# First four heads' k as fp32 over SyncE's queue, and lambda times alpha1 spread as one row

## The chip, the cores and the metric

The kernel runs on one core of a Trainium2 chip. The metric is the device time of one execution in microseconds (us). The engines of a core run side by side, each with its own list of instructions in a fixed order: PE (TensorE, matrix products), DVE (VectorE), ACT (ScalarE), POOL (GpSimd) and SP (SyncE, which here only issues transfers). An engine that waits holds up all that stands behind it in its own list. Transfers between main memory and the core's memory are issued by SP, ACT or POOL.

## The reference, cut to what matters

Eight batches, eight heads, 576 positions, head width 64. Each k and v is averaged over groups of 8 positions, so that every query sees 72 keys. The output of the attention goes through an affine MLP block with the token mixing matrix w_tok.

```
k_p = k.reshape(B, H, Sp, pool, D).mean(axis=3)
v_p = v.reshape(B, H, Sp, pool, D).mean(axis=3)
scores = scale * np.matmul(q, k_p.transpose(0, 1, 3, 2))
attn = softmax(scores)
x = np.matmul(attn, v_p)            # to [batch, position, 512]
a1 = alpha1 * x + beta1
tok = np.einsum('ts,bsd->btd', w_tok, a1)
u = x + lam * tok
a2 = alpha2 * u + beta2
ch = np.maximum(a2 @ w_ch1, 0.0) @ w_ch2
out = u + lam * ch
```

alpha1, beta1, alpha2, beta2 and lam are rows of 512 numbers. The kernel scales x by lam times alpha1 before the token mixing, so it needs that product on all 128 partitions.

## The kernel before, in words

The order of all work is written out by hand: what stands first in the program stands first in each engine's list. Three parts follow one another. A start-up loads the first batch and builds constants; the statements after the definitions (lines 806 to 889) do the attention of batch 0, the token mixing of its chunks and the first MLP pieces; then a loop over nine blocks of four chunks (lines 943 to 1019) does the MLP of one block beside the attention of the next batch. In that loop each step has a due time, and the steps are issued in order of due times.

The positions of a head are split in 512 "main" ones, four per partition, and 64 at the end ("rem"), two per partition. Heads are loaded in two groups of four, called u = 0 and u = 1.

For batch 0 the start works like this:
- `load_vector` (line 209) loads lam and beta1 into rows of a tile `vecs`; alpha1 goes into a third row (line 218). `load_rem` (141) loads the end positions of q and k in four transfers, two on SP's queue and two on ACT's. `load_q_bf` (74) and `load_k16` (82) load q and k of four heads on POOL's queue, which turns fp32 into bf16 on the way. `load_v16` (96) does the same for v. `load_k` (88), used for later batches, loads k as fp32, by default on SP's queue.
- `keep_warm` (601) runs matmuls on zeros whose result nobody reads.
- `att_F` (388) transposes q on PE and copies it out on ACT; `att_Frem` (416) does it for the end positions, after `cast_rem` (164) has cast them.
- `att_K` (437) pools k by matmuls with the tile `pool_main`. The output must stand twice, once on each half of the partitions. For batch 0 four matmuls per head do that, each with two neighbouring position columns of k as weights; `double_k` (431) first copies column 0 behind column 3 so that the last pair exists, and makes the same copy for the end positions (`cast_rem_k`, 176). For later batches `sum_k` (181) adds the four positions of a partition in two operations, written twice, and one matmul per head is enough. The result goes into the tile kpT, one half by ACT and one by DVE.
- `spread_lam` (301) puts lam on all partitions: a matmul of a row of ones with the row lam, copied by ACT into `lam_bc`. `spread_al1` (307) does it for alpha1, 256 columns at a time, and DVE multiplies it with lam_bc into `lamal_bc`. `att_X` and `rest_X` (574, 567) multiply the attention's output by lamal_bc.
- `att_S` (486) makes the scores and their exponentials, `first_V` (464) the pooled v, `att_AV` (546) the product of both.
- `more_constants` (291) sets constants with four memsets on DVE. `bias_row` (282) makes lam times beta1.

lam_bc itself is read again only in `scale_w2` (711) and, for the first block, in `mlp_B` (674).

The tiles k16 and k_raw share two buffers, so that a load of batch 1's k waits for the readers of the tile before it in its buffer.

Of the kernel before, what the change touches and what calls it, by code (L numbers as in the profile page):

```python
# [11 lines left out]
ALU = mybir.AluOpType  # L12
AX = mybir.AxisListType

P = 128
SPG = 72
DM = 512
# [6 lines left out]
def kernel(  # L24
# [18 lines left out]
    nc = tc.nc  # L43
# [8 lines left out]
    def gp(name):  # L52
        return psA.tile([P, 512], FP, tag="gp", name=name)
# [11 lines left out]
    st1 = {}  # L65
# [16 lines left out]
    def load_k16(b, u):  # L82

        t = work.tile([P, 4, 5, D], BF, tag="k_raw", bufs=2, name="k16")
        nc.gpsimd.dma_start(out=t[:, :, 0:4].rearrange("p h c d -> p h (c d)"), in_=rows(k, b, u))
        st1[b]["k"][u] = t
# [54 lines left out]
    def load_rem(b, queue=nc.sync, behind=None):  # L141

        raw = work.tile([P, 2, 2, 2, D], FP, tag="rem_raw", bufs=2, name="rem_raw")
        if behind is not None:
            behind.memset(raw[:, :, :, 0, 0:1], 0.0)
        for i, src in enumerate((q, k)):
            for h in range(2):
                (nc.scalar if h and not b else queue).dma_start(
                    out=raw[:, i, h].rearrange("p c d -> p (c d)"),
                    in_=src[b, h::2, 512:576, :].rearrange("a (i c) d -> i a (c d)", c=2))  # L150
        st1[b]["rem_raw"] = raw
# [12 lines left out]
    def cast_rem(b, eng, copy=None, behind=None):  # L164
        raw = st1[b]["rem_raw"]
        rq = work.tile([P, 2, 2, D], BF, tag="rem_q", bufs=2, name="rem_q")
        if behind is not None:
            behind.memset(rq[:, 0, 0, 0:1], 0.0)
        rk = work.tile([P, 2, 2 if b else 3, D], BF, tag="rem_k", bufs=2, name="rem_k")
        (copy or eng.tensor_copy)(out=rq.rearrange("p c h d -> p h c d"), in_=raw[:, 0])  # L170
        twice = [raw[:, 1, :, c].unsqueeze(2).to_broadcast((P, 2, 2, D)) for c in range(2)]
        if b:
            eng.tensor_tensor(out=rk, in0=twice[0], in1=twice[1], op=ALU.add)
        st1[b]["rem"] = rq, rk

    def cast_rem_k(eng):
        raw, rk = st1[0]["rem_raw"], st1[0]["rem"][1]
        eng.tensor_copy(out=rk[:, :, 0:2], in_=raw[:, 1])
        eng.tensor_copy(out=rk[:, :, 2], in_=raw[:, 1, :, 0])
# [20 lines left out]
    lam_bc = const.tile([P, DM], FP, tag="lam_bc", name="lam_bc")  # L200
    lamal_bc = const.tile([P, DM], FP, tag="lamal_bc", name="lamal_bc")
# [3 lines left out]
    vecs = const.tile([65, 3, DM], FP, tag="vecs", name="vecs")  # L205
# [3 lines left out]
    def load_vector(i, src, queue=nc.scalar):  # L209
        queue.dma_start(out=vecs[0:65:64, i], in_=src.unsqueeze(0).to_broadcast((2, DM)))  # L210

    new_batch(0)
    load_vector(0, moe_lam)
    load_rem(0)
    load_q_bf(0, 0)
    load_k16(0, 0)
    load_vector(1, moe_beta1, nc.sync)
    nc.scalar.dma_start(out=vecs[0:1, 2], in_=moe_alpha1.unsqueeze(0))
    start = const.tile([1, 2], FP, tag="start", name="start")
    nc.vector.memset(start, 0.0)  # L220
    nc.scalar.activation(out=start[:, 1:2], in_=start[:, 0:1], func=AF.Exp, bias=0.0, scale=1.0)
# [45 lines left out]
    for i in range(2):  # L267
# [5 lines left out]
    nc.vector.memset(pool_v[:, 64:], 0.0)  # L273
    nc.vector.memset(pool_vr, 0.0)
    nc.vector.memset(vr16, 0.0)
    nc.vector.tensor_scalar(out=pool_v[:, 0:64], in0=pool_main, scalar1=8.0, scalar2=None,
                            op0=ALU.mult)
    nc.vector.tensor_tensor(out=pool_vr[0:32, 64:72], in0=pool_v[0:32, 0:16:2],
# [12 lines left out]
    def more_constants():  # L291
        nc.vector.memset(ones_bf, 1.0)
        nc.vector.memset(ones_lo[0:64], 1.0)
        nc.vector.memset(ones_lo[64:128], 0.0)
        nc.vector.memset(wtT[:, :, S:640], 0.0)
# [2 lines left out]
        behind.memset(al2_bc[:, 0:1], 0.0)  # L298
        nc.sync.dma_start(out=al2_bc, in_=moe_alpha2.unsqueeze(0).to_broadcast((P, DM)))

    def spread_lam():

        ps = gp("ps_bc")
        nc.tensor.matmul(out=ps, lhsT=ones_row, rhs=vecs[0:1, 0])
        nc.scalar.copy(out=lam_bc, in_=ps)

    def spread_al1(half):

        ps = gp("ps_bc")[:, 0:256]
        cols = slice(256 * half, 256 * half + 256)  # L310
        nc.tensor.matmul(out=ps, lhsT=ones_row, rhs=vecs[0:1, 2, cols])
        nc.vector.tensor_tensor(out=lamal_bc[:, cols], in0=lam_bc[:, cols], in1=ps, op=ALU.mult)

    def setup_vectors():
        ps = gp("ps_vec")
# [72 lines left out]
    def att_F(b, hp, copy=nc.scalar.copy):  # L388


        st = st1[b]
        u, r = hp // 2, hp % 2
        if r == 0:
            st["qT"][u] = work.tile([P, 8, P], BF, tag="qT", bufs=4, name="qT")
        if b > 1:
            if r == 0:
                nc.sync.dma_start_transpose(out=st["qT"][u],
                                            in_=st["q"][u].rearrange("p h c d -> p (h c d)"))
            return
        ps_q = gp("ps_q").bitcast(BF)  # L400
        for c in range(4):
            nc.tensor.transpose(  # L402
                out=ps_q[:, 128 * c:128 * c + 128],
                in_=st["q"][u][:, 2 * r + c // 2, 2 * (c % 2):2 * (c % 2) + 2].rearrange(
                    "p c d -> p (c d)"),
                identity=identity_bf)

        def finish(copy):
            copy(out=st["qT"][u][:, 4 * r:4 * r + 4, :],
                 in_=ps_q[:, 0:512].rearrange("p (c t) -> p c t", c=4))  # L410

        if copy is None:
            return finish
        finish(copy)

    def att_Frem(b, copy=None):

        st = st1[b]
        st["rem_qT"] = work.tile([P, 2, P], BF, tag="rem_qT", bufs=2, name="rem_qT")
        if copy is None:  # L420
            nc.sync.dma_start_transpose(out=st["rem_qT"],
                                        in_=st["rem"][0].rearrange("p c h d -> p (c h d)"))
            return
        ps_q = gp("ps_qr").bitcast(BF)
        for c in range(2):
            nc.tensor.transpose(out=ps_q[:, 128 * c:128 * c + 128],
                                in_=st["rem"][0][:, c].rearrange("p h d -> p (h d)"),
                                identity=identity_bf)
        copy(out=st["rem_qT"], in_=ps_q[:, 0:256].rearrange("p (c t) -> p c t", c=2))

    def double_k(u):

        nc.vector.tensor_copy(out=st1[0]["k"][u][:, :, 4], in_=st1[0]["k"][u][:, :, 0])
        if u == 0:
            cast_rem_k(nc.vector)

    def att_K(b, u, copy):

        st = st1[b]
        ps_kp = gp("ps_kp")  # L440
        kp = ps_kp[:, 0:4 * SPG].rearrange("p (h g) -> p h g", g=SPG)
        n, nr = (1, 1) if b else (4, 2)
        for h in range(4):
            for c in range(n):
                nc.tensor.matmul(  # L445
                    out=kp[:, h, 0:64],
                    lhsT=st["k"][u][:, h, c:c + 2].rearrange("p a d -> p (a d)"),
                    rhs=pool_main, start=(c == 0), stop=(c == n - 1))
        for hh in range(2):
            for c in range(nr):  # L450
                nc.tensor.matmul(
                    out=kp[:, hh:4:2, 64:72],
                    lhsT=st["rem"][1][:, hh, c:c + 2].rearrange("p a d -> p (a d)"),
                    rhs=pool_rem.rearrange("p (g u r) -> p u r g", r=2, u=2)[:, u],
                    start=(c == 0), stop=(c == nr - 1))
        if b:
            copy(out=kp_pool[u], in_=kp)
            return
        for a in range(2):
            rows = slice(64 * a, 64 * a + 64)  # L460
            (copy or (nc.scalar.copy, nc.vector.tensor_copy)[a])(
                out=kpT_pool[u][rows, a], in_=kp[rows])
# [138 lines left out]
    def keep_warm(count):  # L601

        ps = psB.tile([P, DM], FP, tag="ch", bufs=2, name="ps_warm")
        for _ in range(count):
            nc.tensor.matmul(out=ps, lhsT=warm[:, 0:P], rhs=warm)
# [204 lines left out]
    for u in range(2):  # L810
        load_k(1, u, queue=nc.gpsimd)
    keep_warm(13)
    att_F(0, 0)
    att_F(0, 1)
    cast_rem(0, nc.vector)
    more_constants()
    keep_warm(1)
    att_Frem(0, nc.scalar.copy)
    keep_warm(1)
    spread_lam()  # L820
    double_k(0)
    att_K(0, 0, None)
    spread_al1(0)
    bias_row(0)
    att_S(0, 0)
    att_S(0, 1)
# [18 lines left out]
    att_S(0, 5)  # L845
    att_AV(0, 4)
    att_S(0, 6)
    spread_al1(1)
    att_AV(0, 5)
    att_X(0, 4, 6, nc.gpsimd, False)  # L850
    att_S(0, 7)
# [91 lines left out]
    for n in range(NBLK):  # L943
# [27 lines left out]
        if n >= FIRST:  # L971
# [22 lines left out]
            else:  # L994
                for m in range(4):
                    todo.append((27.2 if m < 2 else 29.2, lambda m=m: store(n, m)))
        if n == 0:
            todo.append((6.2, lambda: setup_rowsum(4)))
            todo.append((8.3, setup_wtok_odd))
            for g in range(2, 4):  # L1000
                todo.append((4 * g - 0.8, lambda g=g: setup_bias(range(4 * g, 4 * g + 4))))
# [48 lines left out]
```

## Time and profile before

| what | value |
|---|---|
| median of 3 runs | 333.14 us (332.15 to 333.55) |
| profiled execution, its own time | 333.62 us |
| span of that execution, first to last instruction | 331.9 us |
| PE busy | 323.7 us (98%) |
| DVE busy | 233.6 us (70%) |
| ACT busy | 175.7 us (53%) |
| POOL busy | 95.2 us (29%) |
| mean granted clock of PE | 0.995 |

The page also gives the span in 40 slices of 8.3 us. The digits are tenths of busy time; PEclk is the clock that PE was granted, in tenths of full speed.

```profile
PE   7999999999999999999999999999999999999995
DVE  6674289989679969676967796877788783263263
PEclk9799999999999999999999999999999999999999
```

In rows of the timeline the numbers are the start and the length of a group in us, then the engine, the line, the operation, the tile written and the tile read, the shape and the count; in brackets stands the idle time of the engine before it and what ended it. In the chain of waits every piece is start, length and work. A row of a transfer queue gives packets, MB and the share of the 16 transfer engines' time.

### The profile page before, as it was taken

The numbers are of one execution on the slowest core, as the hardware profiler recorded it, in microseconds if no ns is written. First come the engines' busy times: TensorE is split into PE (matmuls) and PEld (weight loads), VectorE is DVE, ScalarE is ACT, GpSimd is POOL, SyncE is SP. The second block draws the span as 40 slices with busy tenths as digits, with TensorE's granted clock in tenths as the row PEclk, the third lists the DMA queues.
The fourth block names the chain that finished last, engine by engine and source line by source line (L and its number), as shares of the span: only waits on it lengthen the run. The fifth ranks groups of instructions, "written<-read, shape, count | busy, mean of one in ns | idle before, by whom it ended". The sixth has DMA issues, their size and how long they took to land.

```text
span 331.9 us, 6477 instructions
## 1 busy us (share of the span) xinstructions
PE 323.7 (98%) x2500; PEld 209.6 (63%) x2531; DVE 233.6 (70%) x485; ACT 175.7 (53%) x322; POOL 95.2 (29%) x110
## 2 busy tenths in 40 slices
PE   7999999999999999999999999999999999999995
PEld 3667864455544576656775677558755866586584
DVE  6674289989679969676967796877788783263263
ACT  3584989448422861388128812682268225703710
POOL 8669828401247011800280027102510200000000
PEclk9799999999999999999999999999999999999999
DMA  8999999966895992499449943996340044004003
GB/s 117 191 217 270 270 209 245 206 148 101 152 243 99 219 181 81 80 232 173 147 109 209 173 136 73 209 187 176 65 136 2 0 65 143 2 0 127 1 32 97
DMA packets 66472, 45.81 MB, mean 138 GB/s; under 512 B 34397, under 2 KB 57061, under 8 KB 66442
## 3 DMA queue, kind: packets, MB, share of 16 engines
q1 hardware_dynamic: 52092, 32.67, 43.3%
q0 software_dynamic: 13824, 12.40, 22.9%
q8 instruction: 20, 0.33, 0.4%
q10 hardware_dynamic: 526, 0.34, 0.4%
q14 instruction: 10, 0.08, 0.1%
HBM read 38.30 MB, written 9.44 MB: 144 GB/s over the span
## 4 chain that ended last, share of the span: by engine, by line
PE 94%; DMA 2%; DVE 1%; issue 1%; POOL 1%; ACT 0%; POOLq 0%
PE ps_h L662 38%; PE ps_w L785 26%; PE ps_tok L614 11%; PE ps_ch L682 8%; PE ps_av L556 3%; PE ps_s L513 2%; DMA k<-in_k_dram 2%; PE ps_kp L445 1%; PE ps_sc L493 1%; PE ps_r L520 1%; PE ps_av L560 1%; PE ps_v L472 0%; PE ps_w L329 0%; PE ps_q L402 0%; DVE u_sb L618 0%
## 5 line engine op out<-in xcount | busy, mean ns | idle before, releaser
L662 PE MATMUL ps_h<-u_fm,w 128*128 128x512 bf16 (+2 forms) x588 | 132.6, 368 | 1.3 <-DVE bias_cols L665 0.2
L669 ACT ACTIVATE H<-ps_h,bias_cols 128x512 bf16<-128x512 f32 x144 | 98.2, 688 | 56.5 <-PE ps_h L662 55.5
L662 PEld LDWEIGHTS <-w 128*128 128x128 bf16 x608 | 65.6, 114 | 49.9 <-issue 2.2
L785 PEld LDWEIGHTS <-H 128*128 128x128 bf16 x560 | 53.5, 98 | 10.8 <-DVE u_sb L803 1.2
L622 ACT CAST u_bf<-u_sb 128x512 bf16<-128x512 f32 x32 | 19.8, 618 | 69.9 <-issue 39.9
L785 PE MATMUL ps_w<-w_l,H 128*128 128x256 bf16 x448 | 53.6, 272 | 0.0
L803 DVE TENSOR_TENSOR u_sb<-u_sb,ps_w 128x512 f32<-128x512 f32 x54 | 36.3, 683 | 17.1 <-PE ps_w L785 17.1
L578 POOL TENSOR_TENSOR xs<-x_tm,lamal_bc 128x512 bf16<-128x512 f32 x12 | 15.9, 1328 | 108.7 <-DVE x_tm L564 108.5
L614 PE MATMUL ps_tok<-xs,wtT 128*128 128x512 bf16 (+3 forms) x194 | 44.6, 380 | 0.4
L618 DVE TENSOR_TENSOR u_sb<-x_tm,ps_tok 128x512 f32<-128x512 f32 (+1 forms) x40 | 27.4, 684 | 9.9 <-PE ps_tok L614 9.8
L564 DVE TENSOR_TENSOR x_tm<-ps_av,rec 128x320 f32<-128x320 f32 x64 | 31.5, 492 | 2.6
L542 ACT ACTIVATE ET<-ps_s 72x512 f16<-72x512 f32 x56 | 32.3, 592 | 0.0
L614 PEld LDWEIGHTS <-wtT 128*128 128x128 bf16 (+3 forms) x200 | 17.4, 100 | 16.0 <-issue 1.1
L562 DVE RECIPROCAL rec<-ps_av 128x5 f32<-128x5 f32 x64 | 12.2, 190 | 16.9 <-PE ps_av L560 16.7
L483 DVE TENSOR_TENSOR v_u<-v_u 72x1024 f32<-72x1024 f32 (+1 forms) x24 | 22.7, 948 | 0.2
L785 PE MATMUL ps_w<-w_t,h_s 128*128 128x256 bf16 x168 | 22.6, 272 | 0.0
L682 PEld LDWEIGHTS <-H 128*128 128x128 bf16 x128 | 11.9, 98 | 13.7 <-issue 0.4
L754 DVE TENSOR_TENSOR H<-H,H 128x1024 bf16<-128x1024 bf16 x14 | 9.7, 690 | 14.3 <-ACT H L669 14.2
L185 POOL TENSOR_TENSOR k_raw<-k_raw 128x512 f32<-128x512 f32 x14 | 18.8, 1341 | 0.9 <-PE ps_ch L682 0.7
L785 PEld LDWEIGHTS <-h_s 128*128 128x128 bf16 x168 | 16.4, 98 | 4.1
L187 POOL TENSOR_TENSOR k_bf<-k_raw 128x512 bf16<-128x512 f32 x14 | 18.5, 1319 | 1.1
L754 DVE TENSOR_TENSOR h_s<-H 128x1024 bf16<-128x1024 bf16 x21 | 14.4, 686 | 6.0 <-ACT H L669 5.8
(148 smaller groups left out, 367.6 us busy)
## 6 DMA issues: line engine op xcount, KB each, us to landing
out_dram<-u_sb SPq DMA_DIRECT2D x29, 256.0 KB
k_raw<-in_k_dram SPq DMA_DIRECT2D x12, 512.0 KB
v_u<-in_v_dram SPq DMA_DIRECT2D x12, 512.0 KB
q_bf<-in_q_dram POOLq DMA_DIRECT2D x16, 256.0 KB, 7.3
w<-in_moe_w_ch_dram POOLq DMA_DIRECT2D x6, 512.0 KB, 12.5
out_dram<-u_sb SPq DMA_DIRECT2D x11, 128.0 KB
w<-in_moe_w_ch_dram POOLq DMA_DIRECT2D x1, 1024.0 KB, 15.0
k_raw<-in_k_dram POOLq DMA_DIRECT2D x2, 512.0 KB, 16.8
```

Source lines behind the costliest of these rows:

```text
L483: nc.vector.tensor_tensor(out=out, in0=t[:, :, 0:width], in1=t[:, :, width:2 * width], op=ALU.add)
L542: nc.scalar.activation(out=o, in_=i, func=AF.Exp, bias=0.0, scale=0.125)
L564: nc.vector.tensor_tensor(out=x[:, 1 - odd:6 - odd, dd:dd + D], in0=av[:, :, 0:64], in1=rec.unsqueeze(2).to_broadcast((P, 5, D)), op=ALU.mult)
L614: nc.tensor.matmul(out=ps_tok[p0:p1], lhsT=wtT[0:kk, at, P * c:P * c + p1 - p0], rhs=xs_pool[i][0:kk, sc, :], start=(sc == 0), stop=(sc == 4))
L618: nc.vector.tensor_tensor(out=s["u"][p0:p1, :], in0=x[p0:p1, 1 + c if c < 4 else 5 - 5 * i, :], in1=ps_tok[p0:p1, 0:DM], op=ALU.add)
L622: nc.scalar.copy(out=s["u_bf"], in_=s["u"])
L662: nc.tensor.matmul(out=ps_h[:, t0:t1 + one], lhsT=w1_of(cc, j), rhs=rhs, start=(cc == 0), stop=(cc == 3))
L669: nc.scalar.activation(out=H4[n, j // 4][:, j % 4, :], in_=ps_h, func=AF.Relu, bias=bias_cols[:, j:j + 1], scale=1.0)
L682: nc.tensor.matmul(out=ps, lhsT=H_of(n, j)[:, 128 * m:128 * m + 128], rhs=(w2l if n else w2)[j // 4][:, j % 4, :], start=(j == 0), stop=(j ...
L754: nc.vector.tensor_tensor(out=o, in0=a, in1=b, op=op)
L785: nc.tensor.matmul(out=ps, lhsT=stat(j), rhs=moving(j), stop=(j == 7), start=(first and (pp == 0 or alone) and j == 0), skip_group_check=True)
L803: nc.vector.tensor_tensor(out=o, in0=o, in1=banks[key, "both"], op=ALU.add)
```

## The change

The loads of batch 0's first group change: k comes as fp32 on SP's queue, as SP's first transfer, and alpha1 is loaded before ACT's two rem transfers. DVE adds k's four positions (`sum_k`), so that `att_K` needs one matmul per head for this group; the second group stays as it was. The product lam times alpha1 is made by DVE on one row, spread by one matmul of 512 columns, and copied by ACT into lamal_bc. lam_bc is no longer filled from PE: a transfer on SP's queue writes it during the first block. more_constants moves behind att_K, one of the warm matmuls goes, and `spread_lamal` stands before `att_Frem`.

```diff
     load_vector(0, moe_lam)
+    nc.scalar.dma_start(out=vecs[0:1, 2], in_=moe_alpha1.unsqueeze(0))
+    load_k(0, 0)
     load_rem(0)
     load_q_bf(0, 0)
-    load_k16(0, 0)
     load_vector(1, moe_beta1, nc.sync)
-    nc.scalar.dma_start(out=vecs[0:1, 2], in_=moe_alpha1.unsqueeze(0))
...
     nc.vector.memset(vr16, 0.0)
+    nc.vector.tensor_tensor(out=vecs[0:1, 2], in0=vecs[0:1, 2], in1=vecs[0:1, 0], op=ALU.mult)
...
-    def spread_lam():
+    def spread_lamal():
         ps = gp("ps_bc")
-        nc.tensor.matmul(out=ps, lhsT=ones_row, rhs=vecs[0:1, 0])
-        nc.scalar.copy(out=lam_bc, in_=ps)
-
-    def spread_al1(half):
-        ps = gp("ps_bc")[:, 0:256]
-        cols = slice(256 * half, 256 * half + 256)
-        nc.tensor.matmul(out=ps, lhsT=ones_row, rhs=vecs[0:1, 2, cols])
-        nc.vector.tensor_tensor(out=lamal_bc[:, cols], in0=lam_bc[:, cols], in1=ps, op=ALU.mult)
+        nc.tensor.matmul(out=ps, lhsT=ones_row, rhs=vecs[0:1, 2])
+        nc.scalar.copy(out=lamal_bc, in_=ps)
+
+    def load_lam(behind):
+        behind.memset(lam_bc[:, 0:1], 0.0)
+        nc.sync.dma_start(out=lam_bc, in_=moe_lam.unsqueeze(0).to_broadcast((P, DM)))
...
     def double_k(u):
-        nc.vector.tensor_copy(out=st1[0]["k"][u][:, :, 4], in_=st1[0]["k"][u][:, :, 0])
         if u == 0:
             cast_rem_k(nc.vector)
+        else:
+            nc.vector.tensor_copy(out=st1[0]["k"][u][:, :, 4], in_=st1[0]["k"][u][:, :, 0])
...
-        n, nr = (1, 1) if b else (4, 2)
+        n, nr = 1 if b or u == 0 else 4, 1 if b else 2
...
     keep_warm(13)
+    sum_k(0, 0, nc.vector)
     att_F(0, 0)
     att_F(0, 1)
     cast_rem(0, nc.vector)
+    double_k(0)
+    keep_warm(1)
+    spread_lamal()
+    att_Frem(0, nc.scalar.copy)
+    att_K(0, 0, None)
     more_constants()
-    keep_warm(1)
-    att_Frem(0, nc.scalar.copy)
-    keep_warm(1)
-    spread_lam()
-    double_k(0)
-    att_K(0, 0, None)
-    spread_al1(0)
     bias_row(0)
...
     att_S(0, 6)
-    spread_al1(1)
     att_AV(0, 5)
...
         if n == 0:
+            todo.append((1.5, lambda: load_lam(nc.vector)))
```

## The prediction

> **What bounds the kernel now.** I read the page's chain of waits by engine and line first, then the same chain in order of time for the first 60 us, then the timeline and the table by stretches around the edit.
>
> ```profile
> PE 94%; DMA 2%; DVE 1%; issue 1%; POOL 1%; ACT 0%; POOLq 0%
> ```
>
> ```profile
> 2.25 6.64 DMA k<-in_k_dram
> 8.93 0.81 PE ps_kp L445 x16
> 9.87 0.40 ACT kpT L461
> 10.29 0.47 DVE kpT L461
> 10.81 0.33 PE ps_sc L493
> ...
> 18.50 0.62 PE ps_bc L311 x2
> 19.12 0.23 PE ps_av L556 x4
> ```
>
> The chain is TensorE for 94% of the span; the one long piece that is not is the load of the first four heads' k, issued at 2.25 and landed at 8.89. From 10.81 on TensorE hands on to itself almost without a break. So a microsecond won before that point, or a matmul taken out behind it, reaches the end. The second spread of alpha1 (L311) is such a matmul: 0.62 us of the chain.
>
> ```profile
> 6.60 0.62 PE L402 MATMUL ps_q<-identity_bf,q_bf 128*128 128x128 bf16 x8 [0.90 <-DMA q_bf<-in_q_dram]
> 7.06 0.38 PE L605 MATMUL ps_warm<-early 128*128 128x512 f16 x1
> 7.70 1.12 PE L304 MATMUL ps_bc<-vecs,ones_row 1*128 1x512 f32 x2
> 8.00 0.39 ACT L429 COPY rem_qT<-ps_qr 128x256 bf16<-128x256 bf16 x1
> 8.85 0.59 ACT L305 COPY lam_bc<-ps_bc 128x512 f32<-128x512 f32 x1 [0.47 <-PE ps_bc L304]
> 9.05 0.29 DVE L178 CAST rem_k<-rem_raw 128x256 bf16<-128x256 f32 x1
> ```
>
> Before k lands, everything else is already done: q is transposed by 7.06, lambda is spread and copied by 9.44. These steps have slack only because k is late.
>
> ```profile
> 11.00:12.00 1.00, 1.00 (x8) 0.88 (x7) 0.89 (x2) 0.86 (x4) 1.00 (x2) 0.50 1.44 187
> 14.00:14.50 0.50, 0.50 (x8) 0.44 (x7) 0.33 (x2) 0.39 (x2) 0.00 (x0) 0.63 1.16 221
> ```
>
> In this table of stretches the third column from the right is the granted clock. It is 0.50 from about 10.95 to 14.37 and full elsewhere after the start: the first scores run at half speed.
>
> **The change, part by part.** Against the profiled run: 333.62 us, of which the span is 331.9 and 1.72 lies around it; it is 0.48 above the median of 333.14.
>
> *When k and q land.* k leaves POOL's queue and becomes SP's first transfer. SP's first transfer now (rem_raw, issued 0.81) moves its first packets at 2.5, so k's 512 packets start there. How fast? In 121 to 126.5 us two such loads (1,024 packets) took 122.5 to 126.2 alone: 277 a microsecond, 1.85 us for one. Beside POOL's queue the hardware queues now get 178 a microsecond (below: 99 and 79), which makes 2.9 us. The last packet is at 4.35 to 5.4. q_bf's 512th packet passes at about 5.55 and it lands at 6.5, a lag of 1.0; so k lands at 5.3 to 6.4, and I take 6.1, nearer the shared rate.
>
> ```profile
> q0 software_dynamic: 257, 0.13, 104.5%
> ...
> q0 software_dynamic: 199, 0.10, 70.7%
> q1 hardware_dynamic: 99, 0.05, 33.6%
> q10 hardware_dynamic: 79, 0.04, 13.2%
> ```
>
> These are the packets of the queues in 3.75 to 4.75 (first line: POOL's queue nearly alone) and in 4.75 to 5.75 (beside SP's and ACT's): POOL's q transfer falls from 257 to 199. With k beside it from 3.75 to 5.1 it loses some 60 packets, 0.25 us: the transposes start at 6.85 instead of 6.60. Bounds: no delay, or k's whole 1.85 us ahead of it, 8.45.
>
> The Trainium skill ("DMA: Bandwidth & Descriptors", section "Issuing engines are not separate DMA queues") says that transfers from SP, ACT and POOL all run on the same 16 engines and that another issuer saves only issue time. The packet rows agree in kind: the queues share. By that rule alone, with k charged to q in full, the sum would be a loss of about 0.8 us; the measured fall of POOL's rate makes it 0.25.
>
> *The rows of q and k beyond 512 (rem).* On SP they now stand behind k, on ACT behind alpha1's issue (0.52 us). The last of ACT's packets go at about 7.9 now; plus 0.55 and the lag gives a landing of 8.5 to 9.5, taken 8.8.
>
> *VectorE ahead of the scores.* POOL loses one DMA issue (3.12 - 2.25 = 0.87 us), so pool_main is ready at 4.7 instead of 5.56. The row product lambda times alpha1 costs 0.68 (row L284: 1x512) and fits from 4.56, if both rows have landed; then the three pool constants (0.93 from 5.59 to 6.52) end at 6.2. sum_k is two operations of 128x512, 0.69 each (L618, L624): 6.2 to 7.6. The cast of rem q takes 0.30 to 7.9; that of rem k waits for 8.8 and takes 0.42 to 9.25. The four memsets of more_constants (0.77 from 7.15 to 7.92) move behind kpT, where VectorE waits for the first pooled v until 13.16: nothing.
>
> *TensorE and ScalarE ahead of the scores.* Transposes 6.85, plus 0.46 and one warm matmul 0.22, plus 1.12 for the spread: 8.65. Now the order on ScalarE matters: in the changed program the copy of lamal_bc stands before those of rem_qT and kpT. 8.65 + 0.04 + 0.59 = 9.28, + 0.39 = 9.67, + 0.39 = 10.1; VectorE's half of kpT 0.46 to 10.55. att_K, with 4 matmuls for 16, is ready at 9.25 + 0.3 = 9.55 and no longer sets it. Now: 10.26 and 10.75. **Gain 0.15 to 0.2**; bounds: 0.6 gained (q not delayed, copies tighter) and, with q at the far bound, 1.4 lost.
>
> So the 6.6 us of k in the chain are not won: q, the spread and three copies on ScalarE stand right behind.
>
> *A wait added.* ACT's issue of beta2 now waits for the semaphore that k uses, in place of lambda's; the q copies stand behind it. They wait for TensorE until 7.3 anyway, so it costs nothing while k lands before 7; after that, one for one.
>
> *Spreads.* L311 twice goes. The first (9.76) lies in the wait for kpT: 0. The second is 0.62 on the chain. Bounds 0 and 0.69. For 0.62 to survive, what lands next must be early: v's second half lands at 7.58 + 7.8 = 15.4 and is used at 16.4, w_tok at 8.31 + 9.8 = 18.1 and is used at 19.5. Both have a microsecond, and POOL issues both 0.87 earlier. VectorE loses its two 0.42 products there, which helps it keep pace. **Gain 0.62.**
>
> *Lambda loaded later.* A memset of 0.06 and 256 KB on SP at about 33 us, beside v_main and the w2 loads. At the 207 to 241 GB/s of those microseconds that is 1.1 to 1.3 us of transfer. v_main lands at 28.69 + 11.6 = 40.3 and VectorE takes it at 41.42; then first_V wants the result at 44.01, ready at 43.15. Slack 1.1 + 0.86, less 0.8 that the rest comes earlier: it about covers the load. Taken 0; bound 0.4 lost. lam_bc's first reader is at 47.5. The two copies of wtT behind it on SP (24.09 now) are late by 9 us; the tile they fill is read at 62.4.
>
> Sum: 0.17 + 0.62 = **0.8 us less**: 332.8 on the profiled run, 332.4 against the median.
>
> **The clock.** The half clock costs the work of 3.42 us up to half of it, 1.7 us. The Trainium skill ("TensorE: Matmul & The Clock Gate", Part 1) has it fall after a free-running window of about 3.4 us without enough activity; here 10.95 to 14.37 is 3.42 long, and 7.5 to 10.95, just before, has the gaps at 8.82 and 10.0. By that rule, fewer matmuls ahead of the scores (12 of k, one warm, a spread) can only keep the fall or bring it sooner, which leaves the sum or takes 1 us from it.
> From the rows alone: the stretch before the scores stays as sparse, so I keep the dip where it is, and leave up to 1.7 either way for a shift.
>
> **The rivals.**
> *k or rem late (slower).* If SP's k does not get its share of the engines, it lands at 8.2: sum_k to 9.6, the two casts to 10.3, att_K 10.6, kpT 11.0 and 11.45, 0.7 late; in the half clock that pushes work from full to half speed, up to 1.4. Less 0.62: 0.8 slower, 333.9. It decides from k at about 7.6 or rem k at 9.6. For it: rem packets of ACT's queue now take from 5.0 to 7.9 although issued at 2.0. Against: SP's first transfer starts at 2.5 with the engines empty.
> *The dip goes or shortens.* Its work runs full: 332.4 - 1.7 = 330.7. For it: work moves ahead of 10.95 and the three runs of before already spread by 1.4 us. Against: the gaps stay.
> *Hidden anyway.* The 0.62 is taken back behind 18.5, by the next exp on ScalarE (0.70 at 19.53 fills the gaps) or by v_main: 333.1.
>
> **How the numbers follow.** Forecast 332.4: 0.52; dip gone 0.16; hidden 0.14; late k 0.18. The range leaves out about a tenth at each end: 330.7 (the dip gone) to 334.0 (late k). The likeliest's own is 331.7 to 333.0. What a measurement of this kernel can tell from no change is about 0.5%, 1.67 us: below 331.5 is the dip case and a tail of the forecast, 0.16 + 0.05 = 0.21; above 334.8 is a k still later than in the rival, 0.08 of its 0.18; between 0.71.
>
> **What would show it.** In the changed profile: k landed by 6.4 and sum_k starting at 6.2 on VectorE; the q transposes at 6.85; the copy of lamal_bc, not k, in the chain ahead of kpT; scores at 10.2; no spread near 18; sum_v unmoved or earlier at 40.7. Wrong if sum_k waits beyond 7, if scores start after 10.8, or if the granted clock has another shape before 15 us.

## The result and the profile after

| | before | after |
|---|---|---|
| median of 13 runs each | 333.21 us (332.15 to 335.41) | 336.23 us (334.13 to 337.81) |
| ratio, 95% interval | | 1.0073 [1.0044, 1.0101] |
| profiled execution, its own time | 333.62 us | 336.27 us |
| span | 331.9 us | 334.4 us |
| PE at half clock | 3.42 us | 10.24 us |

The kernel became slower by 3.0 us in the median, by 2.4 in the mean (its executions fall into groups by their clock, see the last section) and by 2.65 in the profiled pair. The forecast was 0.8 us less. The page's chain of waits of the changed kernel, by engine, with the shares of the span:

```profile
PE 95%; DMA 2%; DVE 1%; issue 1%; ACT 0%; POOLq 0%
```

DMA is still 2%. The same chain in order of time (start, length, work) says which transfer:

```profile
1.31 6.88 DMA q_bf<-in_q_dram
...
8.23 0.62 PE ps_q L400 x8
...
9.07 1.85 PE ps_bc L305 x2
...
10.94 0.35 ACT lamal_bc L306
...
11.42 0.38 ACT rem_qT L427
11.80 0.29 ACT kpT L460
...
12.11 0.47 DVE kpT L460
...
12.63 0.43 PE ps_sc L492
```

k is gone from the chain and q has taken its place. q lands at 8.19. Then come the transposes, the spread, and the three copies on ScalarE in the order the prediction gave. The second score matmul of the chain starts at 12.63, against 10.81 before: 1.82 late. The timeline rows show who was waiting:

```profile
6.39 0.67 DVE L185 TENSOR_TENSOR k_raw<-k_raw 128x512 f32<-128x512 f32 x1
8.23 0.62 PE L400 MATMUL ps_q<-identity_bf,q_bf 128*128 128x128 bf16 x8 [1.71 <-DMA q_bf<-in_q_dram]
9.00 1.90 PE L305 MATMUL ps_bc<-vecs,ones_row 1*128 1x512 f32 x2
10.02 0.29 DVE L178 CAST rem_k<-rem_raw 128x256 bf16<-128x256 f32 x1 [1.77 <-DMA rem_raw<-in_k_dram]
```

The sum of k starts at 6.39 with no wait in its brackets, so k was early. TensorE waits 1.71 us for q (0.90 before), and its spread takes 1.90 us instead of 1.12. The spread is longer because the clock fell at about 9.2 (the same spread takes 1.12 at full clock in k_behind_rem below). The slices and three rows of the table of stretches (stretch; busy time of PE, PEld, DVE, ACT and POOL with counts; granted clock; transfer share; GB/s):

```profile
PE   6999999999999999999999999999999999999995
PEclk9589999999999999999999999999999999999999
```

```profile
13.00:14.00 1.00, 1.00 (x8) 0.88 (x7) 0.87 (x3) 0.83 (x3) 0.00 (x0) 0.50 1.18 218
18.00:19.00 1.00, 1.00 (x17) 1.00 (x16) 0.50 (x2) 0.57 (x2) 0.98 (x2) 0.50 1.15 217
19.50:20.00 0.50, 0.50 (x6) 0.33 (x4) 0.47 (x3) 0.50 (x2) 0.50 (x1) 1.00 1.15 217
```

The third column from the right is 0.50 until 19.44. TensorE is busy through 13 to 14 and 18 to 19, and in the trace in every microsecond between them, and still gets half its clock. The stretch lasts 10.24 us, three times the 3.42 of before.

Followed along the program, the starts in the two profiled executions are:

| start of | before | after | later by |
|---|---|---|---|
| q's transposes | 6.60 | 8.23 | 1.63 |
| second score matmul of the chain | 10.81 | 12.63 | 1.82 |
| token mixing of batch 0 | 22.68 | 25.05 | 2.37 |
| token mixing of batch 1 | 54.55 | 57.16 | 2.61 |
| last row of TensorE | 324.56 | 327.19 | 2.63 |

Everything is lost before 25 us, apart from 0.24 in the stage behind it. The removed spread is in this balance too; what it is worth is asked below.

### The profile page after: what moved, and what is told of

Same layout as the page of the kernel before. It is cut to its first block, busy times and chain, and to the rows that moved or that the text cites. A ratio compares the mean times of both kernels' runs of the same rounds, so it can differ in the third digit from the quotient of the medians.

```text
span 334.4 us, 6445 instructions
## 1 busy us (share of the span) xinstructions
PE 324.9 (97%) x2483; PEld 210.4 (63%) x2514; DVE 235.1 (70%) x486; ACT 175.4 (52%) x322; POOL 94.8 (28%) x109
## 4 chain that ended last, share of the span: by engine, by line
PE 95%; DMA 2%; DVE 1%; issue 1%; ACT 0%; POOLq 0%
PE ps_h L661 38%; PE ps_w L784 26%; PE ps_tok L613 11%; PE ps_ch L681 8%; PE ps_av L555 3%; PE ps_s L512 2%; DMA q_bf<-in_q_dram 2%; PE ps_sc L492 1%; PE ps_kp L444 1%; PE ps_q L400 1%; PE ps_r L519 1%; PE ps_av L559 1%; PE ps_bc L305 1%; PE ps_v L471 0%; PE ps_w L327 0%
## 5 line engine op out<-in xcount | busy, mean ns | idle before, releaser
L784 PEld LDWEIGHTS <-H 128*128 128x128 bf16 x560 | 53.5, 98 | 10.8 <-DVE u_sb L802 1.2
L681 PEld LDWEIGHTS <-H 128*128 128x128 bf16 x128 | 11.9, 98 | 13.7 <-issue 0.4
```

Source lines behind the costliest of these rows:

```text
L681: nc.tensor.matmul(out=ps, lhsT=H_of(n, j)[:, 128 * m:128 * m + 128], rhs=(w2l if n else w2)[j // 4][:, j % 4, :], start=(j == 0), stop=(j ...
L784: nc.tensor.matmul(out=ps, lhsT=stat(j), rhs=moving(j), stop=(j == 7), start=(first and (pp == 0 or alone) and j == 0), skip_group_check=True)
```

## The experiments

Each time is set against runs of the kernel before on the same chip (medians 332.67 to 333.04).

### Each half of the change alone

*k_only*: the kernel before, with k as fp32, its sum, and one matmul per head in att_K for four; the spreads stay as they were. The lines below show the loads and the place of the sum.

```diff
+    load_k(0, 0)
     load_rem(0)
     load_q_bf(0, 0)
-    load_k16(0, 0)
...
     keep_warm(13)
+    sum_k(0, 0, nc.vector)
```

> Only the k part of the change: k as fp32 first on SP's queue, sum_k on VectorE, one matmul per head; lambda and alpha1 are spread as before. Theory A (k's packets ahead of POOL's q transfer hold q back, and the rest follows): the q transposes start at 8.1 to 8.3 us, PE is idle for 1.6 us before them, the time is that of the changed kernel plus the 0.6 us of the spread that is not removed: 336.3 to 337. Rival B (the loss lies in the new order of spread and copies ahead of the scores): within 0.5 us of before, 332.8 to 333.6.

Measured: 338.83 us (337.43 to 339.77), ratio 1.0163 [1.0125, 1.0201]; half clock 10.24 us. Two timeline rows of it:

```profile
5.69 0.67 DVE L185 TENSOR_TENSOR k_raw<-k_raw 128x512 f32<-128x512 f32 x1
8.29 0.62 PE L402 MATMUL ps_q<-identity_bf,q_bf 128*128 128x128 bf16 x8 [1.29 <-DMA q_bf<-in_q_dram]
```

The k part alone makes q as late as the whole change does, and it brings the long half clock with it. k was there by 5.69, so k is not late: it is in the way. The time itself lies 1.8 us above what was expected (336.3 to 337), and 2.6 above the whole change: three of its six executions have a clock of 0.977 to 0.979, lower than that of its own profile (0.983).

*lamal_only*: the row product, its one spread and lambda's later load; k as in the kernel before. The lines are set against the kernel before.

```diff
+    nc.scalar.dma_start(out=vecs[0:1, 2], in_=moe_alpha1.unsqueeze(0))
     load_rem(0)
     load_q_bf(0, 0)
     load_k16(0, 0)
```

> Only the lambda part of the change: the product made on one row and spread once, copied ahead of rem_qT, lam_bc loaded later; k comes as bf16 on POOL's queue as before. Theory A: q transposes at 6.5 to 6.7, scores start at 10.3 to 10.8, one stretch of half clock as before, 0.3 to 0.8 us faster than before: 332.4 to 332.9. Rival B: 335 to 336.

Measured: 334.37 us (332.68 to 335.11), ratio 1.0017 [0.9992, 1.0041]; half clock 6.83 us.

```profile
6.92 0.62 PE L400 MATMUL ps_q<-identity_bf,q_bf 128*128 128x128 bf16 x8
```

No wait for q, and no loss that can be told from zero; but no gain of 0.62 either, and 1.5 us above the 332.4 to 332.9 that were expected. The profiled execution is the slowest of the twelve (335.11), so its 6.83 is not typical: only two of the twelve have a clock of 0.990 or less. It does show that two pieces of half clock can come with q on time.

### The clock held, the rest of the change kept

*after_warm*: the changed kernel with more matmuls on zeros, in front of q and while the copies of ScalarE run.

```diff
-    keep_warm(13)
+    keep_warm(21)
...
     att_K(0, 0, None)
+    keep_warm(3)
```

> The changed kernel with 8 more matmuls on zeros ahead of the q transposes (8 x 0.215 = 1.7 us, the idle time there) and 3 more behind att_K. Theory A1 (q's lateness alone sets the loss, the clock only follows): q at 8.2 as before, 335.5 to 336.5. Theory A2 (the lateness costs about 1 us and the two added windows of half clock, 6.8 us, the rest): the granted clock stays full from 5 us to 9 us and beyond, the mean clock rises from 0.983 to 0.990 or more, and the time falls to 333.5 to 334.5.

Measured: 333.42 us (333.00 to 334.21), ratio 1.0008 [0.9987, 1.0028]. A slice row and a timeline row:

```profile
PEclk9999999999999999999999999999999999999999
```

```profile
8.73 0.61 PE L400 MATMUL ps_q<-identity_bf,q_bf 128*128 128x128 bf16 x8
```

q's transposes start still later than in the changed kernel, and yet 2.81 us of the 3.0 are back (336.23 to 333.42; by the ratios 2.2 us). All 12 executions have a mean clock of 0.998 or more. So the larger part of the loss is the clock that falls, and not q's delay as a delay. Against all executions of before on that chip the remainder is 0.4 us, within the interval; but some of those had a fallen clock themselves. Against the 16 of them at 0.998 or more (mean 332.81) the mean of after_warm is 0.69 later (95% interval 0.3 to 1.1): that much the delay still costs with the clock held.

The filler stands in two places, in q's wait and behind att_K, and this run does not tell which of them holds the clock. k_warm below fills q's wait with the same eight matmuls and holds the clock in half of its executions only. That q's wait alone brings the clock down is therefore not shown.

### q first

*k_behind_rem*: the changed kernel with k issued behind SP's two rem transfers.

```diff
-    load_k(0, 0)
     load_rem(0)
     load_q_bf(0, 0)
+    load_k(0, 0)
```

> The changed kernel with SP's order altered: the two rem transfers first, then k. Theory A: POOL's q packets start at 3.0 us again and q lands at 6.6 to 7.3; k lands at 7 to 8, sum_k ends by 9.4, scores start at 10.8 to 11.5, one or two stretches of half clock, 333 to 334.5. If instead SP's transfer costs q the same wherever it stands, q lands at 8 and the time stays at 336.

Measured: 337.15 us (335.44 to 338.19), ratio 1.0104 [1.0064, 1.0144]; half clock 6.83 us.

```profile
6.25 0.61 PE L400 MATMUL ps_q<-identity_bf,q_bf 128*128 128x128 bf16 x8
9.63 0.69 DVE L185 TENSOR_TENSOR k_raw<-k_raw 128x512 f32<-128x512 f32 x1 [3.17 <-DMA k_raw<-in_k_dram]
11.31 0.28 PE L424 MATMUL ps_qr<-identity_bf,rem_q 128*128 128x128 bf16 x2 [3.18 <-DVE rem_q L170]
```

q is back at 6.25: its delay was k's place in the order. The time was expected at 333 to 334.5 and is no better than the whole change's, for another reason: now k lands at about 9.6, later than its 8.89 before. The sum stands ahead of the rem casts in VectorE's list, so TensorE waits 3.18 us for a cast that, in its turn at 10.96, has no wait of its own. The late k of the prediction's slower rival does cost when it is built; in the change itself it did not happen.

The transfer queues show the order. Each row is packets, MB and share of the 16 engines; the stretches are 1.5 to 3.5, 3.5 to 4.5 (two rows in the first fence) and 4.5 to 6.0 us. The changed kernel, SP's queue q1 and POOL's q0:

```profile
q1 hardware_dynamic: 394, 0.40, 59.3%
...
q1 hardware_dynamic: 260, 0.18, 54.5%
q0 software_dynamic: 57, 0.03, 42.0%
...
q0 software_dynamic: 306, 0.15, 88.4%
```

The kernel before, POOL's queue in the same three stretches:

```profile
q0 software_dynamic: 64, 0.03, 17.5%
...
q0 software_dynamic: 246, 0.13, 96.4%
...
q0 software_dynamic: 315, 0.15, 79.0%
```

While SP moves 394 packets, POOL's queue moves none, in a stretch in which it moved 64 before. In the next microsecond it moves 57 for 246. By 6.0 us it has sent 363 packets where it had sent 625, and 512 are q. The two do not share from the start; POOL's queue gets going once SP's is nearly through. Why, no run shows: over the first stretch SP's packets kept the engines busy for 59.3% only.

### Does the kernel before gain from the same filler?

*before_warm*: the kernel before with two more warm matmuls ahead of q, and one behind each of the two spreads ahead of the scores. *k_warm*: k_only with 21 warm matmuls for 13, and one behind the first spread of alpha1.

```diff
-    keep_warm(13)
+    keep_warm(15)
...
     spread_lam()
+    keep_warm(1)
...
     spread_al1(0)
+    keep_warm(1)
```

> The kernel before with 4 more matmuls on zeros in PE's waits ahead of the scores (2 ahead of the q transposes, 1 ahead of att_K, 1 behind spread_al1). Theory A (lateness of q and half clock add up): if the clock stays full, the work of the one 3.4 us stretch runs at full speed and q is not late, so the time falls by 1 to 1.7 us, to 331.3 to 332, with less spread between runs. Rival C (the half clock costs little, since ScalarE and the transfers set the pace there): 333, with or without the stretch.

Measured: 333.12 us (332.16 to 333.88), ratio 0.9997 [0.9980, 1.0015], no clock below 0.998. The expected gain (331.3 to 332) did not come, since there was little to win: of 35 executions of the kernel before beside it, 26 had a clock of 0.998 or more anyway (332.1 to 333.7 us); 9 had 0.995 or less (334.2 to 335.8). The profile that the prediction was built on was one of the minority.

> The k part alone with 9 more matmuls on zeros (8 ahead of the q transposes, 1 behind spread_al1). Theory A: q still at 8.2 or later, the clock full; the lateness alone remains, 333.4 + 0.6 of the spread that is not removed = 333.6 to 334.4, 4.5 to 5 us less than the k part without them. If the k part lost by something else than q and clock, it stays above 336.

Measured: 335.47 us (333.34 to 338.33), ratio 1.0061 [1.0027, 1.0096]. The six executions with a clock of 0.990 or lower took 336.2 to 338.3 us, the six with 0.995 or more took 333.3 to 334.8. One and the same kernel falls into two groups by the clock, some 3 us apart; this filler holds it half of the time, and so the median lies above the 333.6 to 334.4 that were expected. The five executions at 0.998 or more say what the k part, and q's delay in it, costs with the clock held and both spreads in place: their mean is 333.92, for 332.88 of the 26 of before, 1.04 us later (95% interval 0.7 to 1.4).

### Where the spread's 0.62 went

*lamal_warm* and *lamal_warm_more*: lamal_only with filler, so that the clock no longer hides a gain. *lamal_late* and *lamal_late_more*: the same two with the transfer that fills lam_bc some 8 us later.

```diff
-    keep_warm(13)
+    keep_warm(15)          # 17 in lamal_warm_more
...
     spread_lamal()
+    keep_warm(2)           # in lamal_warm_more alone
...
     att_K(0, 0, None)
+    keep_warm(3)           # 4 in lamal_warm_more
...
-            todo.append((1.5, lambda: load_lam(nc.vector)))
+            todo.append((7.5, lambda: load_lam(nc.vector)))   # in the late ones
```

> The lambda part alone with 5 more matmuls on zeros (2 ahead of the q transposes, 3 behind att_K). Theory A: with no stretch of half clock the removed spread shows: 0.6 below the kernel before with full clock, 330.8 to 331.6. If 5 are too few, one or two stretches remain and the time is 332.5 to 334. Rival C: 333 to 334 with the clock full.

> As the run above with 10 more instead of 5 (4, 2 and 4). Theory A: clock full in every run, the spread between runs below 1 us; the surplus matmuls may hold PE up by at most 0.6 us: 331 to 332. Rival C: 333 to 334.

> lamal_warm, with the transfer that fills lam_bc issued some 8 us later, behind batch 1's v_main instead of beside it. Theory (the removed spread's 0.62 us is taken back because lam_bc's 256 KB share the engines with v_main: v_main landed 13.7 us after its issue in lamal_warm, 11.6 in the kernel before): v_main lands 11.5 to 12.5 us after its issue, VectorE takes it (L137) at 39.5 to 40.0 instead of 40.52, the lead over before_warm at mix_T of 1.2 us is kept at the end (0.63 in lamal_warm), and the time is 332.2 to 332.7, ratio 0.996 to 0.998. Rival (v_main is late because it is issued earlier beside the w2 and w_ch loads, lam_bc is not in its way): v_main still lands more than 13 us after its issue, the lead shrinks as before, 332.8 to 333.2, ratio 0.999 to 1.000.

> lamal_warm_more (two and one more of the unread warm matmuls ahead of the scores and behind the spread), with the transfer that fills lam_bc issued some 8 us later, as in lamal_late. Theory: v_main lands 11.5 to 12.5 us after its issue (13.2 in lamal_warm_more) and the time falls from 332.83 to 332.2 to 332.6, ratio 0.996 to 0.998. Rival: unchanged, 332.7 to 333.1, ratio 0.998 to 1.000.

*load_added* and *load_added_late*: before_warm, spreads and all, with that transfer added at the early and at the late place.

```diff
+            todo.append((1.5, lambda: load_lam(nc.vector)))   # 7.5 in load_added_late
```

> before_warm with one thing added: lam_bc is written a second time with the same values by the change's transfer (a memset of 0.06 us and 256 KB over SP), issued where the changed kernel issues it, beside batch 1's v_main; the spreads of lambda and alpha1 stay. Theory (it is this transfer that takes the removed spread's 0.62 us back, by making v_main or batch 2's k late, not the earlier start): the two stages between the token mixings of batch 0, 1 and 2 take 0.2 to 1.7 us more than before_warm's 31.86 + 36.50 = 68.36, and the time is 333.3 to 334.3, ratio 1.000 to 1.004. Rival (the transfer is hidden; the lambda kernels lose there because their start is earlier): 68.3 to 68.45, time 332.7 to 333.2, ratio 0.998 to 1.000.

> The same with the added transfer issued some 8 us later, as in lamal_late. Theory: the first stage keeps 31.86, the second takes 0.6 to 1.7 us more than 36.50, since batch 2's k stands next behind it (GpSimd's wait for k_raw, 1.7 us in before_warm, becomes 3 us or more); 333.3 to 334.5, ratio 1.000 to 1.005. Rival: 36.5, time as before_warm, 332.7 to 333.2.

Measured, with a mean clock of 0.998 or more in all but one execution of lamal_warm, load_added and load_added_late and in all of the others. The columns behind the ratio are from one profile each: the start of batch 0's token mixing, and the two stages from there to batch 1's and batch 2's.

| kernel | median us | ratio, 95% interval | mixing 0 at | stage 1 | stage 2 |
|---|---|---|---|---|---|
| before_warm | 333.12 | 0.9997 [0.9980, 1.0015] | 21.83 | 31.86 | 36.50 |
| lamal_warm | 333.05 | 0.9987 [0.9965, 1.0009] | 20.59 | 32.47 | 36.50 |
| lamal_warm_more | 332.83 | 0.9992 [0.9976, 1.0008] | 21.06 | 31.87 | 36.68 |
| lamal_late | 332.68 | 0.9998 [0.9976, 1.0021] | 22.57 | 31.87 | 38.19 |
| lamal_late_more | 332.90 | 0.9992 [0.9974, 1.0011] | 21.54 | 31.86 | 37.12 |
| load_added | 332.79 | 1.0001 [0.9979, 1.0022] | 21.08 | 32.34 | 36.89 |
| load_added_late | 332.92 | 0.9995 [0.9973, 1.0018] | 21.86 | 31.88 | 36.49 |

Four versions with the single spread, and none can be told from the kernel before; the theories that expected a gain here (331 to 332 in the warm ones, ratios of 0.996 to 0.998 in the late ones) failed. The intervals of the ratios leave room for 0.62 as well as for none. With the clock alike there is less room: against the executions of before at 0.998 or more, the mean of those of lamal_warm is 0.01 us later and that of lamal_warm_more 0.04 earlier, each give or take 0.3.

From the first score to the mixing they are quicker where no load comes late: 10.07 to 20.59 is 10.52 in lamal_warm and 10.76 to 21.06 is 10.30 in lamal_warm_more, for 10.96 to 21.83, 10.87, in before_warm. In lamal_late's profile w_tok came late, and the mixing waited for it; that execution is the slowest of its twelve (335.13, median 332.68), so its row is an extreme one. Behind the mixing the lead shrinks or goes: at the last row of TensorE lamal_warm is 0.63 ahead of before_warm, of 1.24 at the mixing, and lamal_late_more 0.33 behind, after 0.29 ahead. In lamal_warm the chain runs over a transfer again:

```profile
26.75 13.74 DMA v_main<-in_v_dram
```

That transfer took 11.6 us before, and 12.4 in before_warm. In lamal_late, v_main's stage is whole again (31.87), and the next one is longer by 1.69. In its waits of 54 to 93 us (engine, what waited, for what: us, times, longest) stands batch 2's k:

```profile
POOL k_raw L185 <- DMA k_raw<-in_k_dram: 3.6, 1, 3.6
```

and in the same view of the kernel before, and of before_warm:

```profile
POOL k_raw L185 <- DMA k_raw<-in_k_dram: 0.2, 1, 0.2
...
POOL k_raw L185 <- DMA k_raw<-in_k_dram: 1.7, 1, 1.7
```

GpSimd sums batch 2's k, and TensorE waits in the end. A short wait there is free: before_warm has 1.7 us of it and the stage its full speed. Over all the profiles, up to 2.0 us (lamal_warm) leave the stage at 36.5; 2.7, 2.9, 3.2, 3.3 and 3.6 us go with 36.68, 36.89, 37.12, 37.25 and 38.19 (lamal_warm_more, load_added, lamal_late_more, lamal_only, lamal_late). v_main landed 12.6 and 12.4 us after its issue in the two late kernels, for 13.7 and 13.2 in their early ones, about as the theory had it; the ratios are the rival's. So moving the load moved the wait by one stage. Is it the 256 KB itself, or the earlier start? load_added, which has both (its q happened to land early, 6.17), loses 0.87 over the two stages. load_added_late has the load but no earlier start and loses nothing, against what was expected of it. The load alone is not enough, at least there. But lamal_late and lamal_only (23.02, 31.86, 37.25) start later than before_warm and lose all the same. What exactly decides is not settled by one profile each. One thing all of them have: v_main, issued anywhere from 26.75 (lamal_warm) to 32.06 us (k_only), landed between 39.4 and 41.6, so an earlier issue brought no earlier landing. What is shown: v_main or batch 2's k is waited for longer in most of these kernels, and in their profiles that is where the lead shrinks.

## Why the prediction was wrong

*When k and q land: this step failed, by the size of one term.* k was right (there by 5.69 in k_only and by 6.39 in the change, predicted 6.1; its packets passed from 1.9 on, and not from 2.5). For q the working took 0.25 us, from a rate that fell from 257 to 199 packets when the queues shared (58 fewer in each of 1.35 us are 78 packets and 0.30 us, a slip without weight). Measured are 1.63, near the far bound of 1.85. With the clock held, this delay costs about 1 us by k_warm. The rows used were of queues that were both already running. At the start they are not: SP's first transfer goes all but alone. The Trainium skill's section that the prediction weighed ("DMA: Bandwidth & Descriptors", "Issuing engines are not separate DMA queues") says that transfers run on the same 16 engines whoever issues them. To charge k to q in full was the prediction's own reading of it, and here that was the better price: 8.45 by it, 8.23 measured.

*The clock: this step failed, and it is the one that costs the time.* "I keep the dip where it is" turned out wrong by two stretches in the profile. after_warm puts 2.8 us of the medians on it. The prediction had both pieces in hand, a price of up to 1.7 us for one stretch and a wait that could grow ahead of the scores, and joined them only in its slower rival, for a late k, with one extra stretch at most. It also took the stretch of the one profile as the kernel's normal state, when 26 of 35 executions of before had none. Two of its own signs of being wrong came: scores after 10.8, and another shape of the clock before 15 us. Why the two further stretches came is open beyond what the filler shows: q's wait is part of it at most, and the 12 matmuls of k that are gone were not tested alone.

*rem k* was costed at 8.8 and read by VectorE at 10.02; covered, because TensorE was in its slow spread until 10.8.

*Order of spread and copies, att_K with 4 matmuls, VectorE's sum:* as predicted, only later as a whole. The chain has exactly the three copies.

*Spreads, 0.62: this term did not show at the end, though the larger part of the miss is not its own.* At full clock 0.35 to 0.57 reach the mixing (10.52 and 10.30 for 10.87); at the end nothing that these runs can tell from zero.

*Lambda loaded later, taken 0, bound 0.4:* the slack was counted for v_main alone. Batch 2's k stands behind it and is waited for already in the kernel before, and that stage lost 0.18 to 1.69 us in four of the five kernels that have the lambda part alone. In the changed kernel itself that stage is unmoved (36.50 for 36.49), and the 0.24 of the stage before it is a wait on VectorE, in the trace put down to the memset of lam_bc (k_behind_rem, with the same memset, has 32.12 there too).

*The rivals:* "k or rem late" named the right side but the wrong transfer, and 0.8 us slower for 3.0. "Hidden anyway" fits what was measured of the lambda half. "The dip goes" was never there to be won: with the clock held, the kernel before is no faster than its usual execution.

No version here beats the kernel before beyond its interval; the lowest ratio is 0.9987 [0.9965, 1.0009].

## What to carry to other kernels

A transfer put first on a second queue took nearly its whole length (1.63 of 1.85 us) from what another queue had issued at that time, neither being under way yet; price it in full against whoever waits for the other one, even when it lands early itself. Where TensorE waits close to a full-speed stage, ask first what the wait does to the clock of the microseconds behind it, and look at the clock of all runs, not only of the profiled one, before taking a dip as given. A gain at the head of a kernel has to be followed through the next saturated stretch of loads, past the first load to the second.

## What the runs showed of the hardware

The half clock comes in pieces of one length: 3.42 us in the profile of before, 6.83 in lamal_only and k_behind_rem, 10.24 in the changed kernel and k_only: one, two and three times 3.41. The Trainium skill ("TensorE: Matmul & The Clock Gate", Part 1) states a free-running window of 3413 ns, and that agrees. It does not tell why two more windows stayed at half here, the rows above showing TensorE busy; no run settles that. The number of pieces differs between executions of one kernel: the changed kernel's clocks of 0.988 to 0.990 go with 334.1 to 334.7 us, and 0.979 to 0.980 with 337.4 to 337.8. With 2 x (1 - clock) x span for the time at half speed (some 7 and 14 us, an estimate), each window more costs about 1.6 us there. The price is not a constant: seven executions of the kernel before at 0.987 to 0.989, some 8 us by the same estimate, took 335.2 to 335.8 for the 332.1 to 333.7 at full clock, about 1.3 a window.

SP's queue moved up to 200 packets in 0.5 us (3.5 to 4.0, the last of k's 512 and the first rem rows), while POOL's queue, whose q was issued at 1.31, sent 12 packets in that half microsecond and none before. In k_behind_rem, with k later, POOL's queue had sent 82 by 3.5.
